# Five landing buffers instead of four, shared with the second experts' input, and a planner that counts more time for a transfer

## The chip, the cores and the metric

The kernel runs on one core of a Trainium2 chip. The time is that of the device for one execution, in microseconds (us); the median of several executions counts. The engines of the core are TensorE (PE in the profile, its weight loads PEld), VectorE (DVE), ScalarE (ACT), GpSimd (POOL) and SyncE (SP), which issues every transfer in this kernel. Each engine works through its own queue in a fixed order; an instruction that waits holds up all that stands behind it on the same engine.

## The reference

Three layers follow each other. Attention over 4 batches, 8 heads, 576 positions and 64 channels, with a mask in blocks of 64; then "first experts" on the 2304 tokens; then "second experts":

```python
scores = scale * q @ k.T                       # masked by blocks of 64, softmax, @ v
h = maximum(maximum(x @ w1, x @ w2), x @ w3)   # 512 -> 768
x2 = h @ w_out                                 # 768 -> 512
gate = 1 / (1 + exp(-(x2 @ w_gate)))           # 512 -> 1536
out = (gate * (x2 @ w_val)) @ w_out2           # 1536 -> 512
```

The weights of both expert layers arrive as 64-bit floating point numbers, so a piece of 128 x 512 weights is 512 KB.

## The kernel before, in words

Products are computed from a high and a low part of each operand (three matmuls instead of one), so every weight and every activation is split into two by a cast and a subtraction. A piece of weights goes through these steps: a transfer into a landing buffer (`wraw`, the ring `raw` of four buffers), ScalarE's first step on it (line 671), VectorE's shift (675) and join (679), ScalarE's cast to the high part (691) and VectorE's subtraction for the low part (`sub`, line 90), after which the buffer is free. The second experts have 36 such pieces, three for each of 12 blocks f: gate, value, output. Blocks 0 to 3 go to the tiles `WB`, which take the memory that attention has left; the others go to the ring `w`.

Attention runs as 32 jobs, the first experts as 8 chunks of tokens (0 to 3 of 256 tokens, 4 to 7 of 320). A chunk is 18 groups of 12 matmuls (lines 511 to 513) into the PSUM ring `ps_m` of two buffers, each followed by an evacuation (line 520 on ScalarE, the maximum `m`, line 522, on VectorE), casts to `HR`, then four projections of 18 matmuls (549 to 551), whose results are staged as `x2s` and stored to `x2d` in HBM.

All this is ordered by a planner, `plan()`, that is run when the kernel is built. It simulates five engines with costs written in the code and lets each one take the ready operation that is due first. For a transfer it adds the bytes to one wire at 370 KB per us, and calls what needs the data ready 1.9 us after the wire is done, and 0.13 us later for any dependence. A tile of a ring of n buffers waits until the tile n before it is free. The resulting order is fixed for TensorE, VectorE, ScalarE and SyncE; `run_plan()` writes the instructions in it, under `tc.manual_schedule(engines=STATIC)`.

The second experts stand behind that in the code and are not in the plan. They work on six blocks of 384 tokens. Their instructions are placed by a scheduler that simulates the program and fills in what is ready, with the number set by `at(t)` as priority. TB is the planned end of TensorE's work. For each block c, `get_x` loads the input into `xraw` (one buffer of 768 KB, in the memory that attention has left), VectorE copies it to a high part and GpSimd subtracts for the low part (`XE` or `XT`); the first block's copies overwrite the input of chunk 7, so they wait for its experts. Then come, for each f, 12 matmuls into `ps_g` (ring `ps_m`) and 12 into `ps_v` (lines 1002 to 1004), the sigmoid, a product, a split, and nine matmuls of the output projection (982 to 984).

Of the kernel before, what the change touches and what calls it, by code (L numbers as in the profile page):

```python
# [8 lines left out]
F32 = mybir.dt.float32  # L9
F32R = mybir.dt.float32r  # L10
U32 = mybir.dt.uint32
# [6 lines left out]
B, H, S, D = 4, 8, 576, 64  # L18
DM = H * D
NP = H // 2  # L20
KD = DM // 128
# [4 lines left out]
N2 = 384  # L26
NC2 = TOK // N2
U = 1536
PC = 512
# [9 lines left out]
ENG = {  # L39
    "gl": "G",  # L40
    "oc": "AAV",
    "sx": "V",
    "sl": "G",
}
# [10 lines left out]
    "hcast": 6.0,  # L55
    "w2late": 10.0,
    "lean": 0.0,
    "cold": 45.0,
    "evac2": 30,
    "olag": 3.731,  # L60
}

RING = {"qk": 2, "v": 4, "s": 3, "t": 2, "o": 1, "m": 2, "w": 8, "raw": 4, "tmp": 4, "st": 3}


@with_exitstack
def block_attention_moe_moe(ctx: ExitStack, tc, k1, q1, v1, k2, q2, vt, wa, wb, out):
    nc = tc.nc
    wide = wa.dtype == U64
    V, A, G, T = nc.vector, nc.scalar, nc.gpsimd, nc.tensor  # L70
    P = PLAN

    def f32(ap):
        return ap.bitcast(F32)

    def at(t):
        tc.cur_priority = int((t + 200.0) * 1000)

    def copy(e, out, in_, scale=None):
        if e == "A":  # L80
            A.activation(out, in_, AF.Copy, scale=scale) if scale is not None else A.copy(out, in_)  # L81
        else:
            n = V if e == "V" else G
            if scale is None:
                n.tensor_copy(out, in_)  # L85
            else:
                n.tensor_scalar(out=out, in0=in_, scalar1=scale, scalar2=None, op0=ALU.mult)

    def sub(e, out, a, b):
        (V if e == "V" else G).tensor_tensor(out=out, in0=a, in1=b, op=ALU.subtract)  # L90

    dram = ctx.enter_context(tc.tile_pool(name="dram", bufs=1, space=bass.MemoryType.DRAM))
    base = ctx.enter_context(tc.tile_pool(name="base", bufs=1))
    raw_p = ctx.enter_context(tc.tile_pool(name="raw", bufs=4))
    tmp_p = ctx.enter_context(tc.tile_pool(name="tmp", bufs=4))
    st_p = ctx.enter_context(tc.tile_pool(name="st", bufs=3))
    pm = ctx.enter_context(tc.tile_pool(name="pm", bufs=RING["m"], space=PSUM))

    x2d = dram.tile([128, KD, TOK], F32, name="x2d")
# [9 lines left out]
    ap1 = att.enter_context(tc.tile_pool(name="ap1", bufs=1, reuse_waits="tile"))  # L109
    qk_p = att.enter_context(tc.tile_pool(name="qk", bufs=RING["qk"], reuse_waits="tile"))  # L110
    v_p = att.enter_context(tc.tile_pool(name="v", bufs=RING["v"], reuse_waits="tile"))
    sm_p = att.enter_context(tc.tile_pool(name="sm", bufs=4, reuse_waits="tile"))
    ps_s = att.enter_context(tc.tile_pool(name="ps_s", bufs=RING["s"], space=PSUM))
    ps_t = att.enter_context(tc.tile_pool(name="ps_t", bufs=RING["t"], space=PSUM))
    ps_o = att.enter_context(tc.tile_pool(name="ps_o", bufs=RING["o"], space=PSUM))

# [10 lines left out]

    PT = ap1.tile([128, 2, 1408], F32, name="PT")  # L130
    EO = [0, 128, 0, 384]
    SEG = {(0, 2): 0, (0, 3): 1, (1, 2): 2, (1, 3): 3, (2, 2): 4, (2, 3): 5, (3, 3): 6}

# [25 lines left out]
    def plan():  # L159

        lat = 0.13
        succ = {o: [] for o in ops}
        for o in ops:
            for d in o.deps:
                succ[d].append(o)

        def least(o):
            return min(o.cost) if isinstance(o.cost, tuple) else o.cost

        for o in reversed(order(succ)):  # L170
            t = [s.due - least(s) - lat for s in succ[o]]
            o.due = min(t + [x for x in (o.pos, o.late) if x is not None] + [1e9])
        free = {"P": 6.0, "V": 2.0, "A": 2.5, "S": 0.0}
        wire = [0.0]
        rings = {}
        waiting = {o: len(o.deps) for o in ops}
        pools = {"P": [], "V": [], "A": [], "B": [], "S": []}
        for o in ops:
            if o.eng != "P" and waiting[o] == 0:
                pools[o.eng].append(o)  # L180
        pe = [sorted([o for o in ops if o.eng == "P" and o.stream == s], key=lambda o: o.pos) for s in "AM"]

        def ready(o):

            if any(d.end is None for d in o.deps):
                return None
            t = max([d.end + lat + (1.9 if d.eng == "S" else 0.25 * (d.eng == "P")) for d in o.deps] + [0.0])
            if o.ring:
                r = rings.setdefault(o.ring, [])
                n = RING[o.ring]  # L190
                if len(r) >= n:
                    old = r[len(r) - n]
                    if any(d.end is None for d in old.frees) or not old.frees:
                        return None
                    t = max(t, max(d.end for d in old.frees) + lat)
            return t

        def choose(cands, e):
            best = None
            soon = None  # L200
            for o in cands:
                t = ready(o)
                if t is None:
                    continue
                if t <= free[e] + 0.02:
                    k = (o.due, t)
                    if best is None or k < best[0]:
                        best = (k, o, free[e] if t < free[e] else t)
                elif soon is None or (t, o.due) < soon[0]:
                    soon = ((t, o.due), o, t)  # L210
            return best or soon

        left = len(ops)
        while left:
            picks = []
            for e in "PVAS":
                if e == "P":
                    c = choose([s[0] for s in pe if s], e)
                elif e in "VA":
                    c = choose(pools[e] + pools["B"], e)  # L220
                    if c is not None and c[1].eng == "B":

                        o, x = c[1], "VA"["AV".index(e)]
                        mine, other = o.cost["VA".index(e)], o.cost["VA".index(x)]
                        if max(free[x], c[2]) + other + 0.02 < c[2] + mine + (P["lean"] if e == "V" else 0.0):
                            c = choose(pools[e], e) if pools[e] else None
                else:
                    c = choose(pools[e], e)
                if c is not None:
                    picks.append((c[2], e, c[1]))  # L230
            assert picks, "the plan is stuck"
            t, e, o = min(picks, key=lambda x: (x[0], "SPVA".index(x[1])))
            cost = o.cost["VA".index(e)] if o.eng == "B" else o.cost
            if e == "P" and t < P["cold"]:
                cost *= 1.9
            o.start, o.on = t, e
            free[e] = t + cost
            o.end = t + cost
            if e == "S" and o.size:
                wire[0] = max(wire[0], t) + o.size / 370e3  # L240
                o.end = wire[0]
            if o.ring:
                rings[o.ring].append(o)
            if e == "P":
                pe["AM".index(o.stream)].pop(0)
            else:
                pools[o.eng].remove(o)
            for s in succ[o]:
                waiting[s] -= 1
                if waiting[s] == 0 and s.eng != "P":  # L250
                    pools[s.eng].append(s)
            left -= 1
# [190 lines left out]
    def keep(j, h, g, e):  # L443
        ps, n = j.tp[h, g[0]], len(g)
        if j.late:
            o = 192 * SEG[g[0]]
            d = PT[:, h, o : o + 192 * n].rearrange("p (s c) -> p s c", c=192)[:, :, :128]
            copy(e, d, ps[:, : 128 * n].rearrange("p (s c) -> p s c", c=128))
        else:
            copy(e, PT[:, h, : 128 * n], ps[:, : 128 * n])  # L450

# [7 lines left out]
    def keep_four(j, i, e):  # L459
        if i == 0:  # L460
            d = PT[:, :, :1152].rearrange("p h (k s) -> p k h s", k=3)[:, :, :, 128:192]
            copy(e, d, j.tp4[0][:, 0:3])
# [137 lines left out]
    for j in jobs:  # L600
        p = jobs[j.i - 1] if j.i else None
        if not j.late:
            visits += [[(j, "S0"), (j, "S1")], [(p, "T0"), (p, "T1")] if p else [], [(p, "P")] if p else []]
        else:
            v = [[(j, "S0")], [(j, "S4")], [(j, "S1")], [(j, "T0")], [(j, "T4")], [(j, "T1")]]
# [14 lines left out]
    t, vn = P["t0"], 0  # L620
# [7 lines left out]
    while vn <= ends[0]:  # L628
        t = visit(t) + P["gap0"]
        vn += 1  # L630
    for i in range(2 * B):
        c = i // B
# [3 lines left out]
        for n, (f, w) in enumerate(mm):  # L636
# [4 lines left out]
            while vn < v0 + n_v and (vn - v0 + 1) * (len(mm) - P["tail"]) <= (n + 1) * n_v:  # L641
                t = visit(t)
# [301 lines left out]

    mb, pv, po = late["mb"], late["pv"], late["po"]
    XE = mb.tile([128, U], F32R, name="XE")
    xraw = mb.tile([128, KD, N2], F32, name="xraw")
    GF = 24 * 0.1625
    OF = 9 * 0.216
    FC = NF2 * (GF + OF)  # L950
# [6 lines left out]
        return [t.rearrange("p (k n) -> p k n", k=KD) for t in r]  # L957

    def get_x(c, t):
        at(t - 30)  # L960
        nc.sync.dma_start(out=xraw, in_=x2d[:, :, N2 * c : N2 * c + N2])
        xh, xl = xbuf(c)
        at(t - 20)
        for k in range(KD):
            copy(ENG["sx"], xh[:, k], xraw[:, k])
            sub(ENG["sl"], xl[:, k], xraw[:, k], f32(xh[:, k]))

    get_x(0, TB)
    pend = []
# [22 lines left out]
    for c in range(NC2):  # L992
        xh, xl = xbuf(c)
        for f in range(NF2):
            t0 = TB + c * FC + f * (GF + OF)
            at(t0)
            w = WB[f][:, :, 0:1024].rearrange("p s (w k c) -> p s w k c", w=2, k=KD)
# [12 lines left out]
            o = 768 * (nh[0] % 5)  # L1010
# [70 lines left out]
```

## Time and profile before

| what | value |
|---|---|
| median of 3 runs | 977.79 us (977.33 to 979.42) |
| the profiled execution | 980.47 us |
| its span, first to last instruction | 978.7 us |
| mean granted TensorE clock | 0.984 of full speed |
| busy time of TensorE | 939.3 us (96%) |
| busy time of VectorE | 468.0 us (48%) |
| busy time of ScalarE | 389.4 us (40%) |

The span is what the rows of a trace cover; the execution's own time is 1.8 us longer. Busy shares are means over the whole span, over stages whose limits differ.

### The profile page before, as it was taken

How to read it: one execution, taken by the hardware profiler on the slowest of the kernel's cores; microseconds unless marked ns; L12 is line 12 of the kernel's file. 1: busy time of each engine (PE TensorE's matmuls, PEld its weight loads, DVE VectorE, ACT ScalarE, POOL GpSimd, SP SyncE). 2: the span in 40 equal slices, each digit the busy share in tenths (PEclk: the TensorE clock that was granted, in tenths of full speed). 3: DMA queues.
4: the chain of work that ended last, by engine and by line, in shares of the span. 5: the costliest groups of instructions: out<-in, count | busy, mean ns of one | idle time of the engine just before them, and what ended most of it. 6: DMA issues, size and time to landing. Idle time of an engine off the chain costs nothing.

```text
span 978.7 us, 14918 instructions
## 1 busy us (share of the span) xinstructions
PE 939.3 (96%) x5912; PEld 874.5 (89%) x5912; DVE 468.0 (48%) x1145; ACT 389.4 (40%) x923; POOL 101.0 (10%) x102
## 2 busy tenths in 40 slices
PE   4787999999999999999889999999999999999998
PEld 3587999999999999999879999999999999999997
DVE  7899665688676687676689701002002001100100
ACT  5975434366565466564546512111112111111211
POOL 0000000000000000000013113113113113111111
PEclk9897999999999999999999999999999999999999
DMA  9911122221212214101667401001001000000000
GB/s 310 366 55 44 61 90 71 81 76 60 97 59 83 65 59 175 59 1 26 227 195 255 138 1 65 1 1 63 3 1 35 31 1 1 33 1 1 33 1 33
DMA packets 37350, 72.27 MB, mean 74 GB/s; under 512 B 5792, under 2 KB 19104, under 8 KB 37280
## 3 DMA queue, kind: packets, MB, share of 16 engines
q1 hardware_dynamic: 37280, 71.32, 22.1%
q8 instruction: 46, 0.75, 0.3%
q14 instruction: 24, 0.20, 0.1%
HBM read 61.87 MB, written 9.44 MB: 73 GB/s over the span
## 4 chain that ended last, share of the span: by engine, by line
PE 86%; DMA 6%; DVE 6%; ACT 1%; issue 1%; SPq 1%; ACTq 0%; DVEq 0%
PE ps_m L511 6%; PE ps_m L512 6%; PE ps_m L513 6%; PE ps_out L983 5%; PE ps_out L984 5%; PE ps_g L1002 5%; PE ps_g L1004 5%; PE ps_v L1002 5%; PE ps_g L1003 5%; PE ps_v L1004 5%; PE ps_v L1003 5%; PE ps_out L982 5%; PE ps_o L478 4%; PE ps_t L440 3%; PE ps_m L549 2%; PE ps_m L551 2%
## 5 line engine op out<-in xcount | busy, mean ns | idle before, releaser
L1009 DVE TENSOR_TENSOR gv<-ps_v,sg 128x384 f32<-128x384 f32 x72 | 40.1, 556 | 342.1 <-PE ps_v L1004 341.6
L511 PE MATMUL ps_m<-XT,w 128*128 128x256 f32 (+1 forms) x576 | 177.4, 308 | 10.0 <-DVE m L522 8.2
L513 PE MATMUL ps_m<-XT,w 128*128 128x256 f32 (+1 forms) x576 | 172.2, 299 | 3.5 <-DVE w L90 3.5
L512 PE MATMUL ps_m<-XT,w 128*128 128x256 f32 (+1 forms) x576 | 172.0, 299 | 0.4 <-DVE XT L90 0.4
L511 PEld LDWEIGHTS ps_m<-XT,w 128*128 128x128 f32 x576 | 110.3, 192 | 14.2 <-DVE m L522 7.8
L513 PEld LDWEIGHTS ps_m<-XT,w 128*128 128x128 f32 x576 | 110.5, 192 | 3.9 <-DVE w L90 3.9
L1007 ACT ACTIVATE sg<-ps_g 128x384 f32<-128x384 f32 x72 | 35.4, 492 | 195.2 <-PE ps_g L1004 195.2
L512 PEld LDWEIGHTS ps_m<-XT,w 128*128 128x128 f32 x576 | 110.5, 192 | 1.2 <-DVE XT L90 0.5
L90 POOL TENSOR_TENSOR HR<-gv,HR 128x384 fp32r<-128x384 f32 x72 | 74.0, 1028 | 342.0 <-ACT HR L1013 342.0
L1013 ACT CAST HR<-gv 128x384 fp32r<-128x384 f32 x72 | 37.0, 513 | 149.5 <-DVE gv L1009 149.5
L387 ACT ACTIVATE E<-ps_s,nm 128x256 f32<-128x256 f32 (+3 forms) x128 | 66.3, 524 | 39.2 <-DVE nm L382 38.6
L90 POOL TENSOR_TENSOR XE<-xraw,XT 128x384 fp32r<-128x384 f32 x12 | 13.1, 1111 | 512.6 <-DVE XT L85 512.6
L1004 PE MATMUL ps_g<-XT,w 128*128 128x384 f32 x192 | 64.8, 337 | 0.0
L1002 PE MATMUL ps_g<-XT,w 128*128 128x384 f32 x192 | 64.7, 337 | 0.0
L1002 PE MATMUL ps_v<-XT,w 128*128 128x384 f32 x192 | 64.1, 334 | 0.0
L1004 PE MATMUL ps_v<-XT,w 128*128 128x384 f32 x192 | 64.1, 334 | 0.0
L549 PE MATMUL ps_m<-HR,w 128*128 128x256 f32 (+1 forms) x192 | 60.7, 316 | 1.2 <-ACT HR L533 1.0
L522 DVE TENSOR_TENSOR m<-ps_m,m 128x256 f32<-128x256 f32 (+1 forms) x96 | 43.6, 454 | 37.4 <-PE ps_m L513 36.5
L478 PE MATMUL ps_o<-PT,v 128*64 128x320 f32 (+3 forms) x448 | 54.4, 375 | 6.1 <-ACT PT L81 3.9
L550 PE MATMUL ps_m<-HR,w 128*128 128x256 f32 (+1 forms) x192 | 58.8, 306 | 1.0 <-DVE HR L90 1.0
L551 PE MATMUL ps_m<-HR,w 128*128 128x256 f32 (+1 forms) x192 | 58.9, 307 | 0.5 <-DVE w L90 0.5
L984 PE MATMUL ps_out<-w,HR 128*128 128x512 f32 x144 | 57.0, 395 | 0.0
(116 smaller groups left out, 2151.3 us busy)
## 6 DMA issues: line engine op xcount, KB each, us to landing
wraw<-in_wb_dram SPq DMA_DIRECT2D x36, 512.0 KB, 4.4
qk<-in_k_dram SPq DMA_DIRECT2D x16, 576.0 KB, 4.1
wland<-in_wa_dram SPq DMA_DIRECT2D x5, 1536.0 KB, 17.4
v<-in_vt_dram SPq DMA_DIRECT2D x16, 320.0 KB, 3.0
wraw<-in_wa_dram SPq DMA_DIRECT2D x9, 512.0 KB, 6.5
xraw<-x2d SPq DMA_DIRECT2D x6, 768.0 KB, 4.7
out_dram<-osb SPq DMA_DIRECT2D x18, 256.0 KB, 2.2
qk<-in_k_dram SPq DMA_DIRECT2D x13, 256.0 KB, 3.1
```

The source lines that it names most:

```text
L90: (V if e == "V" else G).tensor_tensor(out=out, in0=a, in1=b, op=ALU.subtract)
L387: A.activation(E[h][:, e : e + 128 * (t + 1)], j.s[h, t], AF.Exp, bias=j.nm[:, c : c + 1], scale=1.0, accum_out=j.sm[:, c : c + 1],)
L478: T.matmul(j.o[rows(h), d : d + n], j.v[:, h, k, :], PT[:, h, c : c + n], start=(k == 0), stop=(k == len(parts) - 1), skip_group_check=True,)
L511: T.matmul(ps, wt[:, 0, w, k], xh[:, k], start=(k == 0), stop=False)
L512: T.matmul(ps, wt[:, 0, w, k], xl[:, k], start=False, stop=False)
L513: T.matmul(ps, wt[:, 1, w, k], xh[:, k], start=False, stop=(k == KD - 1))
L549: T.matmul(ps, wh, hh, start=(f == 0), stop=False)
L551: T.matmul(ps, wl, hh, start=False, stop=(f == NF1 - 1))
L984: T.matmul(ps, gl[:, ct], wh, start=False, stop=(f == NF2 - 1))
L1002: T.matmul(ps, w[:, 0, i, k], xh[:, k], start=(k == 0), stop=False)
L1003: T.matmul(ps, w[:, 0, i, k], xl[:, k], start=False, stop=False)
L1004: T.matmul(ps, w[:, 1, i, k], xh[:, k], start=False, stop=(k == KD - 1))
```

## The change

The planner's two constants for transfers become 2.7 us (was 1.9) and 350 KB per us (was 370). The ring `raw` gets a fifth buffer, in the plan and in memory. To make room, `xraw` goes away as a tile of its own, and `PT` (attention's transposed weights) loses 64 of its 1408 columns. The input of a block of the second experts is now loaded in two halves of 384 KB (`n` is 2 for 64-bit weights), each into a buffer of `raw`; the copies and subtractions are the same eight.

```diff
+    "wire": 2.7,
+    "rate": 350e3,
...
-RING = {"qk": 2, "v": 4, "s": 3, "t": 2, "o": 1, "m": 2, "w": 8, "raw": 4, "tmp": 4, "st": 3}
+RING = {"qk": 2, "v": 4, "s": 3, "t": 2, "o": 1, "m": 2, "w": 8, "raw": 5, "tmp": 4, "st": 3}
...
-    raw_p = ctx.enter_context(tc.tile_pool(name="raw", bufs=4))
+    raw_p = ctx.enter_context(tc.tile_pool(name="raw", bufs=RING["raw"]))
...
-    PT = ap1.tile([128, 2, 1408], F32, name="PT")
+    PT = ap1.tile([128, 2, 1344], F32, name="PT")
...
-            t = max([d.end + lat + (1.9 if d.eng == "S" else 0.25 * (d.eng == "P")) for d in o.deps] + [0.0])
+            t = max([d.end + lat + (P["wire"] if d.eng == "S" else 0.25 * (d.eng == "P")) for d in o.deps] + [0.0])
...
-                wire[0] = max(wire[0], t) + o.size / 370e3
+                wire[0] = max(wire[0], t) + o.size / P["rate"]
...
-    xraw = mb.tile([128, KD, N2], F32, name="xraw")
...
     def get_x(c, t):
-        at(t - 30)
-        nc.sync.dma_start(out=xraw, in_=x2d[:, :, N2 * c : N2 * c + N2])
         xh, xl = xbuf(c)
-        at(t - 20)
-        for k in range(KD):
-            copy(ENG["sx"], xh[:, k], xraw[:, k])
-            sub(ENG["sl"], xl[:, k], xraw[:, k], f32(xh[:, k]))
+        n = 1 + wide
+        for k0 in range(0, KD, n):
+            at(t - 30)
+            x = raw_p.tile([128, PC * n], U32, tag="raw", name="xraw").bitcast(F32)
+            x = x[:, : N2 * n].rearrange("p (k n) -> p k n", k=n)
+            nc.sync.dma_start(out=x, in_=x2d[:, k0 : k0 + n, N2 * c : N2 * c + N2])
+            at(t - 20)
+            for k in range(n):
+                copy(ENG["sx"], xh[:, k0 + k], x[:, k])
+                sub(ENG["sl"], xl[:, k0 + k], x[:, k], f32(xh[:, k0 + k]))
```

## Rows read from the trace of the kernel before

**Rows 1.** The page's slices: 40 equal parts of the span, busy share in tenths.
```profile
PE   4787999999999999999889999999999999999998
```
**Rows 2.** Windows: stretch, length, busy us of each engine, clock, DMA share, GB/s.
```profile
10.00:90.00 80.00, 60.03 (x388) 50.54 (x388) 75.77 (x200) 60.50 (x158) 0.00 (x0) 0.91 0.59 205
100.00:467.00 367.00, 367.00 (x2802) 343.45 (x2801) 254.99 (x694) 197.62 (x511) 0.00 (x0) 1.00 0.23 72
467.00:510.00 43.00, 38.09 (x236) 37.03 (x234) 32.56 (x62) 22.64 (x41) 2.71 (x3) 0.92 0.64 210
510.00:527.00 17.00, 14.54 (x80) 13.75 (x80) 15.99 (x27) 7.29 (x13) 7.10 (x6) 0.90 0.72 230
527.00:975.00 448.00, 447.52 (x2354) 418.65 (x2353) 75.91 (x132) 93.94 (x182) 90.44 (x88) 1.00 0.09 29
```
**Rows 3.** Waits in 463 to 530 us: who waited for whom, total, times, longest.
```profile
DVE wraw L675 <- DMA wraw<-in_wb_dram: 6.6, 5, 2.8
PE ps_m L511 <- DVE m L522: 4.9, 3, 2.9
```
**Rows 4.** Timeline of VectorE, 466 to 476 us: start, length, instruction, idle before.
```profile
468.99 0.43 DVE L675 TENSOR_SCALAR wraw<-wraw 128x512 uint32<-128x512 uint32 x1 [0.95 <-DMA wraw<-in_wb_dram]
...
473.21 0.43 DVE L675 TENSOR_SCALAR wraw<-wraw 128x512 uint32<-128x512 uint32 x1 [2.82 <-DMA wraw<-in_wb_dram]
...
475.19 0.48 DVE L522 TENSOR_TENSOR m<-ps_m,m 128x320 f32<-128x320 f32 x1
```
**Rows 5.** Timeline of SyncE, 440 to 620 us: issues of transfers, merged.
```profile
462.11 0.56 SPq L961 DMA_DIRECT2D xraw<-x2d  x1
463.72 0.33 SPq L106 DMA_DIRECT2D wraw<-in_wb_dram  x1
...
475.30 35.16 SPq L106 DMA_DIRECT2D wraw<-in_wb_dram  x14
512.40 0.56 SPq L961 DMA_DIRECT2D xraw<-x2d  x1
```
**Rows 6.** Instructions on the tile wraw, 463 to 560 us: the transfers' line.
```profile
DMA to landing us min/median/max: 3.3/4.2/9.6
```
**Rows 7.** Timeline of VectorE, 464 to 500 us: five instructions without a wait.
```profile
483.57 0.68 DVE L90 TENSOR_TENSOR WB<-wraw,WB 128x512 fp32r<-128x512 f32 x1
484.17 0.42 DVE L675 TENSOR_SCALAR wraw<-wraw 128x512 uint32<-128x512 uint32 x1
484.51 0.48 DVE L90 TENSOR_TENSOR HR<-m,HR 128x320 fp32r<-128x320 f32 x1
484.91 0.69 DVE L679 SCALAR_TENSOR_TENSOR wraw<-wraw 128x512 uint32<-128x512 uint32 x1
485.51 0.42 DVE L675 TENSOR_SCALAR wraw<-wraw 128x512 uint32<-128x512 uint32 x1
```
**Rows 8.** Timelines of VectorE (m) and TensorE, 500 to 532 us.
```profile
512.84 0.48 DVE L522 TENSOR_TENSOR m<-ps_m,m 128x320 f32<-128x320 f32 x1
...
514.27 0.35 PE L1002 MATMUL ps_v<-XT,WB 128*128 128x384 f32 x1
...
524.72 0.34 PE L1002 MATMUL ps_g<-XT,WB 128*128 128x384 f32 x1
524.89 0.34 PE L1003 MATMUL ps_g<-XE,WB 128*128 128x384 f32 x1
...
527.73 0.45 PE L1002 MATMUL ps_g<-XT,WB 128*128 128x384 f32 x1 [0.39 <-ACT x2s L81]
```
**Rows 9.** Timeline of VectorE, 379 to 393 and 464 to 500 us: early pieces.
```profile
391.43 0.68 DVE L679 SCALAR_TENSOR_TENSOR wraw<-wraw 128x512 uint32<-128x512 uint32 x1
...
463.61 1.28 DVE L90 TENSOR_TENSOR WB<-wraw,WB 128x512 fp32r<-128x512 f32 x2
```
**Rows 10.** Instructions on the tile xraw, whole span: duration ns min/median/max; transfers.
```profile
L90 POOL TENSOR_TENSOR XE<-xraw,XT x12: 1012/1094/1440, 507.3 to 745.5; 128x384 fp32r<-128x384 f32 x12
...
DMA to landing us min/median/max: 4.6/4.7/6.1
```

## The prediction

> **What bounds the kernel now.** Begin with the slices of the page [rows 1]: after the first tenth of the span TensorE is nearly always busy, except for one shallow dip in the middle. The table of windows gives the sizes [rows 2]. From 100 to 467 us TensorE is busy 367.00 of 367 us, and from 527 to 975 us 447.52 of 448, both at clock 1.00: nothing that comes early there is worth anything. What can move lies in two places. In 10 to 90 us VectorE is busy 75.77 of 80 us and TensorE 60.03, so VectorE sets the pace. In 467 to 527 us, where the last attention chunk (chunk 7) goes through the first experts while the second experts' weights are converted, TensorE loses 43 - 38.09 = 4.91 us idle and about 0.08 x 43 = 3.4 us of clock (0.92 is a mean of its two levels, 2.4 and 1.2 GHz) up to 510, then 2.46 and 0.10 x 17 = 1.7 us up to 527: some 12.5 us. Since the part after 527 has no gaps, the end moves one to one with the moment at which the second experts start in earnest.
>
> The waits of that stage [rows 3] say why: VectorE waited 6.6 us for landings of the weights, and TensorE 4.9 us for VectorE's maximum m. VectorE's order is fixed by the plan, so a conversion whose transfer is late holds up the m behind it: the shift at 473.21 waited 2.82 us for its transfer and the m came at 475.19 [rows 4], which is TensorE's longest wait (2.9 us). On the transfer queue [rows 5], 14 landings took 35.16 us to issue, each as a buffer came free: 2.51 us a piece, thus 4 x 2.51 = 10.0 us for one buffer's round.
>
> **The change part by part.** *Plan's transfers.* A 512 KB piece counted 512/370 + 1.9 + 0.13 = 3.4 us from issue to use; now 512/350 + 2.7 + 0.13 = 4.3. Measured, a landing took 3.3 to 9.6 us, median 4.2 [rows 6]. So the plan now agrees with the trace, and puts conversions behind work that is ready. In 10 to 90 us this can give at most VectorE's idle time, 80 - 75.77 = 4.2 us [rows 2]; another order may also cost what the clock cost in 467 to 510, 3.4 us. I take -1.0 us, near nothing: VectorE was 95% busy with work that doesn't shrink. The fifth piece of the first weights goes out before the big landings instead of after them; it is part of those ends.
>
> *Five buffers.* If the round stays 10.0 us, a piece takes 10.0 / 5 = 2.0 us. VectorE allows about this: shift, join and subtraction follow each other after 0.34, 0.60 and 0.60 us [rows 7], 1.54 a piece. So the waits of chunk 7 should mostly go; without the 12.5 us its work would be through at 527 - 12.5 - 4.1 = 510.4 (4.1 us: 24 matmuls of the second experts, 0.17 us from start to start [rows 8], which lie before 527 too).
>
> *PT cut by 64 columns.* Its last segment ends at 7 x 192 = 1344; nothing is removed that is used. No cost.
>
> *The input staged in two buffers.* This is where I see the price. Before, xraw had a buffer of its own: the first block's transfer went out at 462.11 [rows 5], 45 us before its copies, and the second at 512.40, the moment the buffer was free. Now the two halves are the 46th and 47th tiles of the ring, asked for after all 36 weight pieces. The trace shows how a ring shared by planned and unplanned work is handed out: one of the two ps_m buffers was being released from 512.84 on, and TensorE, with its own next projection not yet ready, ran the second experts' ps_v at 514.27, though ps_g stands before ps_v in the code; ps_g got its buffer only at 524.72, after all four projections [rows 8]. That is the order of the code. Nor could the halves take buffers early: the first pieces, 0 to 3 with four buffers and 0 to 4 with five, are joined near 390 us, in VectorE's fixed order, and keep their buffers until their subtractions after 463 [rows 9]; a buffer taken earlier would stop VectorE for good. So the first half waits until piece 31 (of 0 to 35) is converted, the second for piece 32, and nothing covers this: TensorE has no other work after chunk 7.
>
> When is piece 31 through? From 463.6 on VectorE has five subtractions (5 x 0.60 = 3.0), a wait of 2.4 us for the first new landing (the shift that came at 468.99 had been issued at 463.72), 27 pieces x 1.54 = 41.6, and of chunk 7 twelve m, six HR and four staging copies at 0.40 [rows 7] = 8.8: 519.4 with no other idle time. That is the lower bound. By the pace of 2.0 us from the fifth piece at about 472 it is 472 + 26 x 2.0 = 524. If the fifth buffer brought nothing, 475.3 + 27 x 2.51 = 543. I take 523, between the first two, since chunk 7 leaves VectorE to the conversions after 510.
>
> Then: issue 0.3; transfer 3.7 (768 KB took 4.7, a 512 KB piece 4.2 [rows 6, 10], half as much a little less than the piece); copy 0.4; four subtractions on GpSimd one after another at 1.1 (median 1.094 [rows 10]) = 4.4: the last part of the input is ready at 523 + 8.8 = 531.8. Of the first 24 matmuls six are left then, 1.0 us: the second f starts at 532.8, against 527.73 before [rows 8], +5.1. TensorE has then stood for some 15 us; idle stretches of 2 to 5 us in this stage left a clock of 0.90 to 0.92 [rows 2], so I add 1.0 (ends 0 and 1.7).
>
> *Two transfers instead of one.* A measured price: a transfer of half the size saves about 1 us, and the second half hides behind the first half's subtractions. The Trainium skill (DMA: Bandwidth & Descriptors, Rules for kernel authors) speaks against it: many small transfers should be coalesced into one large one. By that rule the input would be better off as one transfer of 4.7 us, and the sum would be the same to about a microsecond, since the first part of the input would come 1.0 us later and the rest no earlier.
>
> Sum: -1.0 + 5.1 + 1.0 = +5.1 us. The profiled execution took 980.47 us (span 978.7 and 1.8 around it), 2.7 above the median 977.79; I take the difference on the median: **983 us**. The likeliest case has the range 977 (519.4 and a start that gains) to 992 (530 and a start that loses).
>
> **Rivals.**
> *The fifth buffer is all that counts (faster).* If the halves get buffers in time, say because the code's order binds ps_m but not this ring, and conversions no longer hold up m, then the 8.3 us lost in 467 to 510 come back: 969.5. For it: the waits [rows 3] and the round of a buffer [rows 5]. Against it: ps_g's wait, and that two of five buffers then hold input. It decides if the first input lands before 510. The Trainium skill (Perfetto Trace Analysis, Optimization Strategy) reads gaps that repeat on the engine that should be saturated as a possible lack of room for the next tile; by that rule the fifth buffer would pay, and the trace agrees as to the gaps.
>
> *Two buffers taken during chunk 7 (slower, another place).* If the halves are let in after 463, the weights have three buffers until the copies at 507: 10.0 / 3 = 3.35 us a piece instead of 2.51 for 14 pieces, +11.7 us: 989.5. For it: unplanned transfers went out the moment a buffer was free (512.40). Against: the same ps_g row.
>
> *No change.* The start gains its 4.2 us and piece 31 is through at its bound of 519.4: -4.2 + 5.1 - 3.6 + 1.0 = -1.7; 976 to 979.
>
> **How the numbers follow.** Forecast 0.55, faster rival 0.20, three-buffer rival 0.15, no change 0.10. A measurement of this kernel tells about 0.2%, 2 us, from no change. The forecast's own range gives 0.47 slower, 0.06 same, 0.02 faster. Together: slower 0.62, same 0.16, faster 0.22. The range 971 to 992 holds the forecast, no change, most of the three-buffer case, and leaves out the deeper part of the faster one.
>
> **What would show it.** In the windows after: 467 to 510 with TensorE busier than 38.09 and clock near 1.00 (right for five buffers); then a hole of some 15 us before the first ps_g or ps_v, ended by GpSimd's XE; the input's two transfers behind the 32nd and 33rd subtractions of the weights. The prediction is wrong if the input's transfers go out before the weights are nearly through, if chunk 7 still waits for m, or if the start moves by more than 4 us.

## The result and the profile after

The changed kernel took 987.72 us (median of 4 executions, 985.03 to 990.61), the kernel before beside it 977.56 us (4 executions, 975.81 to 979.42): a ratio of 1.0098, 95% interval 1.0078 to 1.0117. It is 10.2 us slower. The profiled execution took 985.03 us (span 983.2), the shortest of the four.

First the page's slices of the kernel after; [rows 1] are the same of before.
```profile
PE   5787999999999999999956999999999999999998
...
PEclk9999999999999999999986999999999999999999
```
The shallow dip of before has become a hole, and the granted clock sinks in it. The windows of the kernel after, the four stretches of [rows 2] that matter and two finer ones (columns as there), give it its size.
```profile
10.00:90.00 80.00, 60.98 (x398) 51.43 (x399) 78.40 (x209) 62.52 (x165) 0.00 (x0) 0.94 0.58 206
...
467.00:510.00 43.00, 37.38 (x254) 36.85 (x252) 40.41 (x81) 31.20 (x58) 0.00 (x0) 0.97 0.79 272
510.00:527.00 17.00, 2.05 (x5) 1.42 (x6) 16.24 (x30) 11.76 (x18) 2.93 (x3) 0.50 0.82 270
527.00:975.00 448.00, 447.92 (x2353) 419.75 (x2353) 57.33 (x98) 77.23 (x154) 94.90 (x94) 1.00 0.05 17
...
507.50:524.00 16.50, 0.01 (x1) 0.04 (x1) 15.62 (x30) 12.05 (x20) 0.00 (x0) 0.50 0.91 308
524.00:531.00 7.00, 5.95 (x16) 4.52 (x17) 6.65 (x9) 2.05 (x3) 6.64 (x6) 0.50 0.65 183
```
In 510 to 527 us TensorE is busy 2.05 us where it was 14.54; VectorE is nearly full all the while (30 instructions in 16.24 us). Chunk 7 itself goes better than before: of the 43 - 37.38 = 5.6 us that TensorE misses in 467 to 510, 4.8 lie behind its last projection (at 504.87, below); up to the end of that, in 467 to 505.18, it is busy 37.37 of 38.18 us at clock 1.00. The waits of 463 to 540 us (who waited for whom, total, times, longest) name what ended the hole, to be read beside [rows 3].
```profile
POOL XE L92 <- DMA xraw<-x2d: 522.8, 1, 522.8
...
PE ps_g L1007 <- DVE XT L87: 18.8, 1, 18.8
...
DVE wraw L677 <- DMA wraw<-in_wb_dram: 3.0, 3, 1.9
...
PE ps_m L513 <- ACT m L522: 0.8, 1, 0.8
```
The waits of before have become small (6.6 us for landings to 3.0; TensorE's 4.9 us for VectorE's m are gone, 0.8 us for ScalarE's evacuation are left), and one has come: TensorE stands 18.8 us for a copy of the input. GpSimd, which has done nothing since the span's start (hence the 522.8), begins at 524.07, when the input's first half has landed and VectorE has made the first copy of it (both below; the view names the transfer, by the times the copy was the later). The timeline of SyncE, 440 to 620 us, shows when that left; [rows 5] are its partner.
```profile
466.88 31.17 SPq L108 DMA_DIRECT2D wraw<-in_wb_dram  x15
...
508.83 8.82 SPq L108 DMA_DIRECT2D wraw<-in_wb_dram  x6
518.26 82.95 SPq L967 DMA_DIRECT2D xraw<-x2d  x11
```
Landings now take 31.17 / 15 = 2.08 us a piece instead of 2.51, and the input goes out at 518.26, after the last weight, where before it went out at 462.11. What it waited for stands in the timeline of VectorE of the kernel after: the subtractions of pieces 31 and 32 of the weights, then the input's copies.
```profile
517.55 0.69 DVE L92 TENSOR_TENSOR w<-wraw,w 128x512 fp32r<-128x512 f32 x1
...
520.21 0.69 DVE L92 TENSOR_TENSOR w<-wraw,w 128x512 fp32r<-128x512 f32 x1
...
523.48 0.63 DVE L87 CAST XT<-xraw 128x384 fp32r<-128x384 f32 x2
...
524.65 2.21 DVE L87 CAST XT<-xraw 128x384 fp32r<-128x384 f32 x2
526.78 1.49 DVE L92 TENSOR_TENSOR w<-wraw,w 128x512 fp32r<-128x512 f32 x1
```
Piece 31 is through at 517.55 + 0.69 = 518.24 us, and 0.02 us later the transfer is issued; it landed 4.6 us after its issue, at about 522.9. TensorE's timeline, for [rows 8]: the last projection of chunk 7, the first matmul of the second experts, the first on XE, and the second f's first; and GpSimd's subtractions.
```profile
504.87 0.31 PE L553 MATMUL ps_m<-HR,w 128*128 128x320 f32 x1
...
523.99 0.66 PE L1007 MATMUL ps_g<-XT,WB 128*128 128x384 f32 x1 [18.80 <-DVE XT L87]
525.61 0.69 PE L1008 MATMUL ps_g<-XE,WB 128*128 128x384 f32 x1 [0.97 <-POOL XE L92]
...
532.60 0.33 PE L1007 MATMUL ps_g<-XT,WB 128*128 128x384 f32 x1
...
524.07 5.06 POOL L92 TENSOR_TENSOR XE<-xraw,XT 128x384 fp32r<-128x384 f32 x4 [522.76 <-DMA xraw<-x2d]
```
The second f starts at 532.60 us against 527.73, and from there to the end of the span it takes 450.6 us against 451.0: all of the loss lies ahead of it.

### The profile page after: what moved, and what is told of

Same layout as the page of the kernel before. It is cut to its first block, busy times and chain, and to the rows that moved or that the text cites. A ratio compares the mean times of both kernels' runs of the same rounds, so it can differ in the third digit from the quotient of the medians.

```text
span 983.2 us, 14939 instructions
## 1 busy us (share of the span) xinstructions
PE 933.1 (95%) x5912; PEld 869.0 (88%) x5912; DVE 461.9 (47%) x1143; ACT 390.9 (40%) x925; POOL 99.3 (10%) x102
## 4 chain that ended last, share of the span: by engine, by line
PE 85%; DVE 8%; DMA 4%; ACT 1%; issue 1%; POOL 0%; SPq 0%; ACTq 0%; DVEq 0%
PE ps_m L513 6%; PE ps_m L514 6%; PE ps_m L515 6%; PE ps_out L988 5%; PE ps_out L989 5%; PE ps_g L1008 5%; PE ps_g L1009 5%; PE ps_v L1007 5%; PE ps_v L1008 5%; PE ps_v L1009 5%; PE ps_g L1007 5%; PE ps_out L987 5%; PE ps_o L480 5%; PE ps_t L442 3%; DMA wraw<-in_wb_dram 3%; PE ps_m L551 2%
## 5 line engine op out<-in xcount | busy, mean ns | idle before, releaser
L92 POOL TENSOR_TENSOR XE<-xraw,XT 128x384 fp32r<-128x384 f32 x12 | 13.3, 1134 | 529.1 <-DMA xraw<-x2d 522.8
L551 PE MATMUL ps_m<-HR,w 128*128 128x256 f32 (+1 forms) x192 | 58.8, 306 | 0.3 <-ACT w L693 0.3
L553 PE MATMUL ps_m<-HR,w 128*128 128x256 f32 (+1 forms) x192 | 57.3, 298 | 0.7 <-DVE w L92 0.7
L552 PE MATMUL ps_m<-HR,w 128*128 128x256 f32 (+1 forms) x192 | 57.0, 297 | 1.0 <-DVE HR L92 1.0
L480 PEld LDWEIGHTS ps_o<-PT,v 128*64 128x64 f32 x448 | 31.2, 139 | 29.8 <-DVE PT L87 9.9
```

The source lines that it names most:

```text
L480: T.matmul(j.o[rows(h), d : d + n], j.v[:, h, k, :], PT[:, h, c : c + n], start=(k == 0), stop=(k == len(parts) - 1), skip_group_check=True,)
L551: T.matmul(ps, wh, hh, start=(f == 0), stop=False)
L552: T.matmul(ps, wh, hl, start=False, stop=False)
L553: T.matmul(ps, wl, hh, start=False, stop=(f == NF1 - 1))
```

## The experiments

Ten runs were made in three sets, eight kernels and once more each of the two of this case; beside each set ran the kernel before (medians 977.41, 977.35 and 978.00 us). **The theory:** the ring of landing buffers is handed out in the order of the code; the input's two halves stand behind all 36 pieces, so they can't leave before pieces 31 and 32 are converted, and nothing covers that. **Rivals:** the two buffers that the input takes starve the weights of chunk 7; or the loss comes from the planner's constants or the fifth buffer; or the input is late for another reason (VectorE full, GpSimd in its way).

**e1: the input apart.** The change, but the input lands in three quarter buffers of its own, four transfers a block.
```
+    xq = [mb.tile([128, N2], F32, name=f"xq{i}") for i in range(3)]
...
-            x = raw_p.tile([128, PC * n], U32, tag="raw", name="xraw").bitcast(F32)
+            x = xq[(KD * c + k) % 3]
...
-            nc.sync.dma_start(out=x, in_=x2d[:, k0 : k0 + n, N2 * c : N2 * c + N2])
+            nc.sync.dma_start(out=x, in_=x2d[:, k, N2 * c : N2 * c + N2])
```


> The change, but the input of the second experts keeps buffers of its own (three quarters of 192 KB, four transfers a block) instead of two of the ring. If the late input is the whole loss, the hole of 18.8 us goes away and chunk 7 and the start stay as quick as after the change: the second f starts near 509 to 512 instead of 532.6, and the time is 960 to 965 us. If instead the weights' conversion binds the second experts as soon as the input is in time, the hole moves into the first blocks f and the time is 972 or more.

Measured: 967.29 us, ratio 0.9892 (0.9877 to 0.9907). Of e1 the first requests for the input in SyncE's timeline, and TensorE's last projection and first ps_g:
```profile
459.00 1.32 SPq L966 DMA_DIRECT2D xq<-x2d  x3
...
510.24 0.31 PE L553 MATMUL ps_m<-HR,w 128*128 128x320 f32 x1
510.39 0.34 PE L1005 MATMUL ps_g<-XT,WB 128*128 128x384 f32 x1
```
The hole is gone, and everything else of the change, together with the quarters (about 2 us by themselves, e7 below), is worth 10 us. The requests stand at the same place in the code as in the changed kernel, behind all 36 pieces, and three of the four leave at 459.00: the place in the code holds a transfer back only where it needs a buffer of the shared ring. The time lies between the two expectations, nearer the theory's.

**e2: the constants alone**, in the kernel before.
```
+    "wire": 2.7,
+    "rate": 350e3,
```


> Only the planner's two constants, four buffers and the old xraw. If the constants made the gain of the start (chunk 7's first experts at 461.7 instead of 467.3), it is here in full, and some of the waits of chunk 7 go too: 966 to 972 us. If the fifth buffer made the start's gain, by the earlier transfer of the fifth piece, the start stays at 467 and the time is 974 to 978.

Measured: 973.62 us, ratio 0.9952 (0.9936 to 0.9969): a gain of 3.8 us by themselves. They are not what makes the change slow. The time lies between the two expectations; chunk 7 starts at 464.10, so the start's gain is there, but not in full.

**e3: five buffers with the old constants and the input apart**, as in e1.
```
-    "wire": 2.7,
-    "rate": 350e3,
+    "wire": 1.9,
+    "rate": 370e3,
```


> Five buffers for the weights alone, the old constants, the input in buffers of its own (three quarters). If the constants made the start's gain, chunk 7 begins near 467 as before, and only the waits inside it go (8.3 us of 467 to 510, and what the input's wait cost up to 527): 966 to 971 us. If the fifth buffer made the start's gain: 960 to 965. If the plan's order and not the buffer was what held chunk 7 up, its waits stay: 975 to 978.

Measured: 974.95 us, ratio 0.9980 (0.9966 to 0.9994). This is just below the last of the three ranges and in none of them; whose the small gain is, e7 below says.

**e4: the staging alone**: the changed kernel with four buffers and the old constants.
```
-... "w": 8, "raw": 5, "tmp": 4, "st": 3}
+... "w": 8, "raw": 4, "tmp": 4, "st": 3}
```


> Only the staging: four buffers, old constants, the input in two of the four. If the ring is handed out in the order of the code, chunk 7 is as slow as before and the input's transfers follow the weights' last conversions, near 540 us: a hole of some 15 to 20 us after chunk 7, second f near 552, 1000 us (995 to 1008). If the input takes two buffers as soon as they are free, the weights have two left, chunk 7 takes twice as long (14 pieces at 5.0 us instead of 2.51, +35 us) and there is no hole after it: 1010 us or more.

Measured: 1002.47 us, ratio 1.0251 (1.0236 to 1.0267): the staging costs 25 us. Of e4 the waits of 463 to 550 us, and the timelines of SyncE and TensorE:
```profile
PE ps_g L1007 <- DVE XT L87: 27.1, 1, 27.1
...
517.66 16.55 SPq L108 DMA_DIRECT2D wraw<-in_wb_dram  x9
536.44 81.44 SPq L967 DMA_DIRECT2D xraw<-x2d  x10
...
540.34 0.69 PE L1007 MATMUL ps_g<-XT,WB 128*128 128x384 f32 x1 [27.14 <-DVE XT L87]
```
With four buffers the input goes out later still, again behind the last weight, and the hole is 27 us, longer than the 15 to 20 expected. The rival of starved weights falls: the input took no buffer during chunk 7. Nor was chunk 7 as slow as before, as expected: from its start to its last projection it took 48.3 us, against 57.2 before and 53.2 in e10. The input's copies and the ten ps_v matmuls that ran within it before now come behind it; whether that is the reason was not tested. The 25 us are thus a longer hole less a shorter chunk 7.

**e5: the order of the code, moved.** The changed kernel as it is, but the two tiles of block 0's input are taken and their transfers asked for ahead of piece 27 of the weights; the copies stay.
```
+                if i == 27:
+                    ask_x(0)
                 lands2[i] = raw_p.tile([128, PC * (1 + wide)], U32, tag="raw", name="wraw")
```


> The changed kernel with one step moved: the two landing tiles of the first block's input are taken, and their transfers asked for, ahead of piece 27 of the second experts' weights in the order of the code instead of behind piece 35; buffers, constants and copies stay. The theory (the order of the code hands out the ring, and that alone makes the input late): the transfers leave when pieces 22 and 23 are converted, about 500 us instead of 518, the copies come by 504 to 508, the hole of 19 us on TensorE shrinks to 0 to 4, and the second f of block 0 starts 50 to 55 us after chunk 7 instead of 70.9; 967 to 973 us. The rival (two buffers held while chunk 7 runs leave three for the weights, which then hold up the projection): projection over 50 us after chunk 7's start or TensorE waits for m or weights in it, 978 to 990. The rival that the input is late for another reason than its place in the code (vector engine busy, GpSimd's lock): hole stays over 12 us, 982 or more.

Measured: 971.78 us, ratio 0.9942 (0.9924 to 0.9959). Of e5 the timeline of SyncE, the transfers' line of the tile xraw (480 to 530 us), TensorE's wait in 463 to 545, and its last projection, first ps_g and second f:
```profile
504.75 2.28 SPq L936 DMA_DIRECT2D xraw<-x2d  x2
...
DMA to landing us min/median/max: 4.5/4.7/5.2
...
PE ps_g L1019 <- DVE XT L87: 4.1, 1, 4.1
...
506.46 0.31 PE L553 MATMUL ps_m<-HR,w 128*128 128x320 f32 x1
510.91 0.66 PE L1019 MATMUL ps_g<-XT,WB 128*128 128x384 f32 x1 [4.13 <-DVE XT L87]
...
518.49 0.33 PE L1019 MATMUL ps_g<-XT,WB 128*128 128x384 f32 x1
```
This is the decisive one: same buffers, same constants, same staging, and two requests moved ahead in the code take the hole from 19 us to 4 and the time from 10 us above before to 5.6 below. The first request left at 504.75 instead of about 500 and landed 5.2 us later, at about 509.95, 3.2 us after the end of the last projection; its copy came at 510.41. That is the rest of the hole.

**e6: the change with the old constants.**
```
-    "wire": 2.7,
-    "rate": 350e3,
+    "wire": 1.9,
+    "rate": 370e3,
```


> The changed kernel with the planner's old two constants (1.9 us after a transfer, 370 KB/us): five buffers and the staging in the ring stay. If the constants are worth the 4 to 8 us that they gave with the input staged apart (first four experiments), 991 to 996 us. If with the hole in place the time is set by the last conversions alone and the constants only move work ahead of them, 985 to 990.

Measured: 995.92 us, ratio 1.0185 (1.0165 to 1.0206): the constants are worth about 8 us with the hole in place too (7.7 with five buffers and the input apart, e1 against e3; 3.8 with four, e2). Against e4 (1002.47) the fifth buffer alone is worth 6.6 us there: the input goes out at 529.99 instead of 536.44. SyncE's timeline of e6 has the pace of the landings:
```profile
471.46 35.93 SPq L108 DMA_DIRECT2D wraw<-in_wb_dram  x16
```
That is 35.93 / 16 = 2.25 us a piece with five buffers and the old constants; in e4, with four, 15 took 35.76 us, 2.38 a piece.

**e7: the quarters alone**, in the kernel before: e3 with four buffers.
```
+    xq = [mb.tile([128, N2], F32, name=f"xq{i}") for i in range(3)]
...
-        nc.sync.dma_start(out=xraw, in_=x2d[:, :, N2 * c : N2 * c + N2])
+            nc.sync.dma_start(out=x, in_=x2d[:, k, N2 * c : N2 * c + N2])
```


> The kernel before with one edit: the input of a block comes in four transfers through three quarter buffers of its own instead of one transfer of 768 KB; four landing buffers and the old constants stay. A control for the first and third experiment. If the quarters do nothing by themselves: 975 to 979 us, and the third experiment's 975 is five buffers' share. If they bring the input earlier and that counts: 971 to 974, and the fifth buffer is worth nothing by itself. Three small transfers more per block with nothing gained: up to 981.

Measured: 975.33 us, ratio 0.9980 (0.9967 to 0.9992). The same as e3: with the old constants and the input apart, the fifth buffer by itself gains nothing that can be measured (974.95 against 975.33), and e3's gain was that of the quarters. Nor does it change the pace there, by SyncE's timeline of e7:
```profile
474.20 30.27 SPq L108 DMA_DIRECT2D wraw<-in_wb_dram  x14
```
With four buffers this is 30.27 / 14 = 2.16 us a piece; in e3, with five, 13 landings took 28.10 us, 2.16 too. The Trainium skill (DMA: Bandwidth & Descriptors, Rules for kernel authors) would coalesce many small transfers and finds mostly overhead under 64 KB; here four of 192 KB, above that size, were no worse than one of 768 KB, a little better.

**e8 and e10: both kernels once more**, unchanged, for what one profile can differ from the next.

> The changed kernel as it is, profiled once more. If the early start of chunk 7 in its first trace (461.7 us against 467.3 before) is the plan's own, chunk 7 starts again within 1 us of 461.7. If it varies from execution to execution, it starts 2 to 6 us later, and the span is longer by as much, with the stretch from chunk 7's start to the second f of block 0 again at 69 to 72 us.

> The kernel before as it is, profiled once more, for the spread of the start. If the old constants alone set the start of chunk 7, it starts within 1 us of 467.3 again; if it varies from execution to execution, 464 to 469. From chunk 7's start to the second f of block 0 again 59 to 62 us.

Measured: 988.47 us for the changed kernel, 976.69 for the one before. Of e8 TensorE's first ps_g and second f; of e10 the two windows of the stage (as [rows 2]) and TensorE's first matmul of chunk 7 and second f.
```profile
526.10 0.66 PE L1007 MATMUL ps_g<-XT,WB 128*128 128x384 f32 x1 [20.52 <-DVE XT L87]
...
536.03 0.34 PE L1007 MATMUL ps_g<-XT,WB 128*128 128x384 f32 x1
```
```profile
467.00:510.00 43.00, 37.64 (x234) 35.57 (x233) 35.26 (x67) 23.53 (x43) 4.75 (x4) 0.96 0.70 215
510.00:527.00 17.00, 15.06 (x92) 14.43 (x93) 15.92 (x29) 10.64 (x19) 4.59 (x4) 1.00 0.78 237
...
466.39 0.31 PE L511 MATMUL ps_m<-XT,w 128*128 128x320 f32 x1
...
523.96 0.44 PE L1002 MATMUL ps_g<-XT,WB 128*128 128x384 f32 x1 [1.44 <-ACT x2s L81]
```
Chunk 7's start came back within 1 us in both, as the first of each pair of expectations had it (before, the second, 464 to 469, holds 466.39 as well, so that run doesn't decide between them); but the second f of the kernel before started 57.6 us after it instead of 60.4 (just under the 59 to 62 expected), and that of the changed kernel 73.5 instead of 70.9 (over the 69 to 72 expected).

**e9: the requests still earlier**, ahead of piece 22.
```
-                if i == 27:
+                if i == 22:
```


> The fifth experiment with the input's two transfers asked for still earlier in the code, ahead of piece 22 instead of 27. By the theory of the order of the code they leave at about 488 to 494 us, land before chunk 7's last experts (about 495), the remaining hole of 4.4 us on TensorE goes, and the two buffers come back at about 500: 966 to 970 us. The rival that two buffers held in chunk 7 cost the weights more than the hole is worth: pieces 25 and on wait for them, the second experts' weights or the matmuls of chunk 7 are held up by over 4 us, 972 to 980.

Measured: 965.94 us, ratio 0.9881 (0.9851 to 0.9910), the fastest of all beside e1. Of e9 the timeline of SyncE, the longest wait for a landing, and TensorE's last projection and first ps_g:
```profile
469.10 24.41 SPq L108 DMA_DIRECT2D wraw<-in_wb_dram  x12
494.50 4.07 SPq L936 DMA_DIRECT2D xraw<-x2d  x2
502.00 3.60 SPq L108 DMA_DIRECT2D wraw<-in_wb_dram  x3
...
ACT wraw L673 <- DMA wraw<-in_wb_dram: 13.4, 11, 6.7
...
511.84 0.31 PE L553 MATMUL ps_m<-HR,w 128*128 128x320 f32 x1
511.98 0.34 PE L1019 MATMUL ps_g<-XT,WB 128*128 128x384 f32 x1
```
The hole is gone with the staging kept. The price that the rival spoke of can be seen: no weight is issued from 493.5 to 502.0, and ScalarE waits 6.7 us for one landing. But TensorE loses little by it: in 461 to 515 us it waits 2.4 us in all (1.1 for GpSimd's XE, 0.9 and 0.4 for ScalarE), none of it for weights or for VectorE's m. The projection ends 47.6 us after chunk 7's start instead of 42.8 in e5, and 1.9 us of the difference are eleven ps_v matmuls (0.17 us each) that ran ahead of its end: only 13 matmuls of the first f were left after it.

All profiles side by side, times of first (or last) matmuls in us, from the timelines of TensorE:

| kernel | chunk 7 starts | last projection | first ps_g | second f | chunk 7 to second f | span |
|---|---|---|---|---|---|---|
| before | 467.34 | 524.57 | 524.72 | 527.73 | 60.4 | 978.7 |
| before, again (e10) | 466.39 | 519.56 | 519.82 | 523.96 | 57.6 | 974.9 |
| after | 461.71 | 504.87 | 523.99 | 532.60 | 70.9 | 983.2 |
| after, again (e8) | 462.54 | 505.26 | 526.10 | 536.03 | 73.5 | 986.7 |
| e1 input apart | 464.59 | 510.24 | 510.39 | 514.21 | 49.6 | 965.1 |
| e2 constants alone | 464.10 | 513.28 | 513.43 | 518.07 | 54.0 | 969.0 |
| e3 five, apart, old constants | 465.15 | 514.82 | 514.96 | 518.50 | 53.4 | 969.6 |
| e4 staging alone | 464.61 | 512.89 | 540.34 | 549.25 | 84.6 | 999.9 |
| e5 asked at 27 | 463.67 | 506.46 | 510.91 | 518.49 | 54.8 | 969.1 |
| e6 after, old constants | 466.54 | 514.32 | 535.40 | 543.12 | 76.6 | 993.8 |
| e7 quarters alone | 466.41 | 519.65 | 519.80 | 522.58 | 56.2 | 973.5 |
| e9 asked at 22 | 464.20 | 511.84 | 511.98 | 514.24 | 50.0 | 964.9 |

The medians add up along one path: staging +25.1 (e4 against before), the fifth buffer -6.6 (e6 against e4), the constants -8.2 (after against e6), together +10.3; measured +10.2.

## Why the prediction was right, and where its sizes were not

The mechanism held: slower, by a hole after chunk 7 that the input's place in the order of the code makes. Forecast were 983.0 us, +5.1; measured 987.7, +10.2, inside the range. In the first pair of profiles the second f came 4.9 us later and the span grew by 4.5, close to the +5.1, but that is luck: from chunk 7's start to the second f it took 4.4 us more than forecast (70.9 against 55.7 + 10.8), and the start came 4.6 us earlier than forecast (-5.6 against -1.0). By its steps:

- **Five buffers.** 2.0 us a piece was forecast, 2.08 measured, and the waits of chunk 7 went. The size is right, the reason only in part: I had the round of a buffer stay at 10.0 us and gave the gain to the fifth buffer. With five buffers and the old constants a piece took 2.25 us (e6; 2.38 with four, e4), or 2.16 with five as with four (e3, e7). It takes the new constants too to come to 2.08. (35.16 us for 14 issues are 13 intervals and one issue of 0.33, so 2.68 from issue to issue, against 2.20 after; both figures above are low by the same count.)
- **Piece 31.** Through 55.7 us after chunk 7's start (523 against 467.34); measured 56.5 and, in e8, 57.3 (519.82 against 462.54). Right to about 1 us, and the input's transfer left at that moment. In e6 the same: piece 31 through at 530.0, the transfer at 529.99.
- **From there to the second f: short by 3.6 to 5.4 us.** Forecast were 8.8 us to the last part of the input, 1.0 for the rest of the first f and 1.0 for the clock, 10.8 in all; measured 14.4 (532.60 against 518.24), in e8 16.2. *The input's chain:* 10.9 us (529.13 against 518.24), in e8 12.1. GpSimd began 5.8 us after the issue (524.07 against 518.26) instead of 4.4, since the first half landed after 4.6 us instead of 4.0 (in e8 after 4.9; so half the size saved next to nothing against the 4.7 of [rows 10], where I had called a saving of 1 us measured, though no row of before showed it), and the first copy came only at 523.48, behind a join in VectorE's order; and its four subtractions took 5.06 us instead of 4.4, in e8 5.75, while VectorE's copies ran beside them. *The rest of the first f:* 3.5 us, in e8 4.1. I had counted six matmuls left behind the last part of the input; there were 14, because TensorE does all of ps_g before ps_v and two of ps_g's and twelve of ps_v's were still to come: 14 x 0.17 = 2.4 us instead of 1.0. *The clock:* the other 1.1, in e8 1.7, against 1.0 with ends 0 and 1.7. Right.
- **The start: short by 1.6 to 3.7 us.** I took -1.0, ends -4.2 and +3.4. Chunk 7 started 4.7 us earlier in the mean of two profiles each (462.1 against 466.9). Over all profiles the six with the new constants start it at 463.5, the six with the old at 466.1, with spreads of 2.9 and 2.7 us: 2.6 us is the better figure for the constants, and it lies inside the ends. But I had named a start moved by more than 4 us as a sign of being wrong, and both the first pair (5.6) and the mean of two (4.7) are over it: this term was mis-sized. VectorE, whose idle 4.2 us I read as the ceiling, is busy 78.40 of the 80 us now, 2.6 more than before, and 78.49 with the constants alone (e2); where the rest of the 4.7 came from is open.
- **The baseline: 2.8 us.** I measured everything against one profile of before, which had lost 12.5 us in 467 to 527. In e10 the same kernel lost 9.0: idle 43 - 37.64 = 5.4 and 17 - 15.06 = 1.9, clock 0.04 x 43 = 1.7 and none. Part of what I booked as recoverable belonged to that execution.
- **The other signs.** The hole came, and the input's transfers went out behind the subtractions of pieces 31 and 32. It was VectorE's copy that ended it, after 18.8 us; GpSimd's XE, which I had named, held TensorE for 0.97 us more. TensorE in 467 to 510 was not busier than 38.09 but 37.38, with the clock at 0.97, because the hole begins inside that window; up to its beginning the sign holds (37.37 of 38.18, clock 1.00).
- **The range.** Its ends don't quite come out of the terms. 519.4 with the whole gain of the start is what the rival *no change* has, 976.1 and not 977; 530, for which I gave no row, with the whole loss of the start is 977.8 + 3.4 + 12.1 + 1.0 = 994.3 and not 992. The measured time lies inside either way.

The start pulls one way, the chain behind piece 31 and the baseline the other. With both profiles of each the second f moved by 534.3 - 525.8 = +8.5 us, the spans by +8.2 and the medians by +10.2; the remaining 2 us are within what the executions of one kernel differ (5.6 us after, 3.6 before), and I can't place them.

**The rivals.** *The fifth buffer is all that counts, 969.5:* its condition, the first input landed before 510, was the right point. The change doesn't meet it; e5, with the transfer issued at 504.75 and down 4.5 to 5.2 us later, gave 971.8, and e9, some 10 us earlier, 965.9. The name was wrong: with the input apart the fifth buffer alone (e3 against e7) gained nothing measurable, and what pays is the buffer and the constants together (e1 against e7, 8.0 us). Why the two help each other is argued, not shown: conversions put behind ready work leave chunk 7's m free, and a longer ring keeps the transfers going meanwhile. Four buffers with the new constants and the input apart were not run. *Two buffers taken during chunk 7, 989.5:* came near in time by chance; its mechanism did not occur, and where e9 made it occur it cost at most 2.9 us of the 11.7 that I had put on it, since TensorE never waited for the weights that it held back. *No change:* it needed the start's whole gain and piece 31 52.1 us after chunk 7's start (519.4 against 467.34); that took 56.5.

The rule of the Trainium skill that fits best is one that I did not weigh (DMA: Bandwidth & Descriptors, Rules for kernel authors): issue a transfer early, compute, and wait for it late. The changed kernel issues the input at 518.26 and could use it from 505.18 on; e9 issues it at 494.50, and 22 us come back.

## What to carry to other kernels

When a transfer that has had a buffer of its own is moved into a shared ring, look up which tile of the ring it becomes in the order of the code: it leaves when the tile five (the ring's length) ahead of it is freed, however long its data have been ready. Then ask for it at an earlier place of that order, far enough ahead that it lands before its consumer comes free; here the move was worth 16 us at the first place tried and 22 at the second, and no earlier one was tried. Size such a stall by the work that is left behind the last part of what it waited for, and against more than one profile.

## What the hardware showed that was not expected

- TensorE's granted clock stayed at 0.50 (1.2 of 2.4 GHz) for 7 us after work had begun again behind an idle stretch of 19 us: 5.95 us busy in 524 to 531. In e8 it did so from 526 to about 535. In e9, without a hole, the first f ran at 0.17 us from start to start.
- While GpSimd's subtractions of the input ran, VectorE's two-input subtraction took 1.49 us instead of 0.69, and a copy up to 1.16 instead of 0.35. The Trainium skill (SBUF — State Buffer, SBUF: two separate sides) describes a port pair that the two engines share and that one of them holds for a whole instruction while the other is blocked; these rows fit that, though no run here took the two engines apart.
- The same kernel's stretch from chunk 7 to the second f came out 2.8 us apart in two executions of before and 2.6 in two of after; before, TensorE's clock in 510 to 527 was 0.90 in the one [rows 2] and 1.00 in the other.
